# One-token attention and MLP on one core: values lag six units instead of five, mask added on VectorE, last batch summed in another PSUM bank, first w_2 group loaded in three pieces of rows

## The chip, the core and the metric

The kernel runs on one core of a Trainium2 chip. The time is device microseconds of one execution. The kernel before took 135.18 us as the median of three runs (134.91 to 135.40). Lower is better. All inputs start in HBM, and the output of 576 numbers ends there.

In the text PE is TensorE, DVE is VectorE, ACT is ScalarE, POOL is GpSimd, and SP is the engine that issues nearly all of the DMAs here.

## The reference

One token x of 576 numbers goes through two branches that a scalar gate mixes.

```
g = sigmoid(sum(x * gate_w))
q = x @ wq                                   # 32 heads of 128
k, v = last 4096 positions of the caches     # 16 kv heads, each shared by 2 query heads
a = softmax(q k^T / sqrt(128)) v, heads side by side, @ wo
b = gelu(x @ w1 + b1) @ w2 + b2              # 576 -> 4608 -> 576
out = g * a + (1 - g) * b
```

Everything is bf16 in HBM. The windows of the k and v caches are 16.8 MB each, and wq, w1, wo and w2 have 4.7 to 5.3 MB each. One execution reads 53.6 MB.

## The kernel before, in words

**Units, batches, tiles.** There are 16 kv heads. One kv head (with its two query heads) is a *unit*, `h` in the code, and four units are a *batch* (`HB = 4`, `NB = 4`). A tile of keys or values holds two units in 2 MB. Two DMAs fill it, one into the even partitions and one into the odd ones (`load_kv`, line 99). Six such buffers exist (`kv_pool`, line 77), and keys, values and later the four groups of w_2 take them in turn. A load waits until the last reader of the buffer's earlier content is done.

**What one unit does.** `transposes(h, i)` (line 228) turns four 128x128 blocks of keys by four matmuls against the identity, for i = 0 to 7. They go to one of three PSUM banks (`ps_t`), and DVE (i = 0, 3, 6) or ACT copies them to SBUF. `scores(h, s)` (line 256) adds four matmuls at a time into the PSUM bank `s_ps`, which collects a whole batch. Partitions and columns of even and odd parity belong to different units, so half of the entries of `s_ps` mean nothing. Before, one matmul at the start of each batch (line 261) writes 0 or -1e30 into the bank as a mask, and the scores add to it. `values(h, i)` (line 330) multiplies the probabilities with the values and adds up a whole batch in the PSUM bank `acc` (`ps_o`, one bank).

**Once for a batch.** `softmax(b)` gives four steps: `row_max` (line 284, DVE), `turn_max` (two small DVE operations around a transpose on PE), `spread` (PE spreads the maximum, ACT takes the exponential out of `s_ps`), and `put` (four transposes and eight DVE copies into `ez`). `heads_out(b)` gives two: `take` (line 348, four DVE operations read `acc` and add its four blocks into `a_s`) and `turn_out` (one matmul and a copy into `o_sb`). `norm` (line 501) sums up the denominators, `sums_start` (line 522) clears the bank in which the output is added.

**The order.** The program is written in the order in which each engine runs it. The loop (line 535) goes over `h`. While unit h is scored, the keys of unit h + 1 are transposed, the softmax steps of a batch that has ended are put between them, and the values of unit h - LAG are multiplied, with LAG = 5 (line 531). The loop runs on for five rounds after the last unit, in which only values, the last softmax and the `heads_out` steps are left. `gelu` (line 459) runs as one block at the end of round 10.

**Loads.** SP issues the DMAs in the order of the program, with at most eight on their way: each DMA waits on a completion counter that the one eight places before it has used. The last in this order are eight of values, two of wo, and six of w_2. The four w_2 groups have 128 rows each, and each row of a group is one run of 10368 bytes in HBM. The last group goes in three pieces of columns (line 587).

**The end.** `ow` (lines 593 to 612) is the attention output as columns. The sums for the output (line 632) are 64 matmuls with wo, then 54 with the w_2 groups 0 to 2. `part_s` (line 640) takes them out of PSUM. The last matmuls (line 651) add them and w_2 group 3 into `y_ps`, `y` (line 664) casts the result, and one DMA of four rows writes it.

Of the kernel before, what the change touches and what calls it, by code (L numbers as in the profile page):

```python
# [16 lines left out]
def kernel(  # L17
# [15 lines left out]
    nc = tc.nc  # L33
# [131 lines left out]
    for o in range(2):  # L165
# [22 lines left out]
    row_e = const.tile([2, P], BF16, name="row_e")  # L188
    nc.vector.tensor_copy(
        out=row_e[:].rearrange("k (a e q) -> k a e q", e=2, q=2),  # L190
        in_=ident[0:2, 0:2].rearrange("k (a e q) -> k a e q", a=1, q=1).to_broadcast(
            [2, P // 4, 2, 2]
        ),
    )
    col_e = const.tile([2, BC * P], BF16, name="col_e")
    nc.vector.tensor_scalar(
        out=col_e[:].rearrange("k (a e) -> k a e", e=2),
        in0=ident[0:2, 0:2].rearrange("k (a e) -> k a e", a=1).to_broadcast([2, BC * P // 2, 2]),
        scalar1=-MASK, scalar2=MASK, op0=ALU.mult, op1=ALU.add,
    )  # L200

# [54 lines left out]
    def scores(h, s):  # L256

        b, ul = h // HB, h % HB
        if ul == 0 and s == 0:
            s_tiles[b] = ps_s.tile([P, BC * P], FP32, name="s_ps", tag="s")  # L260
            nc.tensor.matmul(
                s_tiles[b][:], lhsT=row_e[:], rhs=col_e[:], start=True, stop=False
            )
        lo = R * (NGR - 1 - 2 * (h % 2) - s)
        for t in range(NQ):
            i = 4 * s + t
            nc.tensor.matmul(  # L267
                s_tiles[b][32 * t : 32 * (t + 1), :],
                lhsT=qz[:, h // 2, lo : lo + 32],
                rhs=kT[h][:, i * BC * P : (i + 1) * BC * P],  # L270
                start=False,
                stop=(ul == HB - 1 and s == 1),
            )

    def softmax(b):

        s_ps = s_tiles[b]
        mx = small.tile([P, 1], FP32, name="mx", tag="mx")
        m8 = small.tile([1, R], FP32, name="m8", tag="m8")
# [4 lines left out]
        def row_max():  # L284
            nc.vector.tensor_reduce(out=mx[:], in_=s_ps[:], axis=AX.X, op=ALU.max)  # L285
# [12 lines left out]
        def spread():  # L298
            mb = ps_m.tile([P, 1], FP32, name="mb", tag="m")
            nc.tensor.matmul(mb[:], lhsT=m_all[:], rhs=ones_ff[0:1, 0:1], start=True, stop=True)  # L300
            nc.vector.tensor_scalar(  # L301
                out=nb[:], in0=mb[:], scalar1=-SCALE, scalar2=None, op0=ALU.mult
            )
            nc.scalar.activation(  # L304
                out=pr[:], in_=s_ps[:], func=ACT.Exp, bias=nb[:, 0:1], scale=SCALE,
                accum_out=sums[:, b : b + 1],
            )

        def put():
            pT = ps_m.tile([P, BC, P], BF16, name="pT", tag="m")  # L310
            for c in range(BC):
                nc.tensor.transpose(  # L312
                    out=pT[:, c, :], in_=pr[:, c * P : (c + 1) * P], identity=ident[:]
                )
            for s in range(NGR):
                for m in range(HB // 2):
                    nc.vector.tensor_copy(  # L317
                        out=ez[:, b % 2, m, NQ * s : NQ * (s + 1), :, RP * m : RP * (m + 1)],
                        in_=pT[:].rearrange("p c (t s r) -> p t c s r", t=NQ, r=R)[
                            :, :, :, s, RP * m : RP * (m + 1)  # L320
                        ],
                    )
# [7 lines left out]
    def values(h, i):  # L330

        b, ul = h // HB, h % HB
        if ul == 0 and i == 0:
            acc[b] = ps_o.tile([P, BC, Dh], FP32, name="acc", tag="o")
# [124 lines left out]
    def gelu():  # L459
        NF = RJ * NG  # L460
        C0 = 0.7978845608028654
        h_r = const.tile([P, 2, FB], FP32, name="h_r")
        nc.vector.tensor_tensor(
            out=h_r[:], in0=h_box[0][:, :, 0:FB], in1=b1_r[:], op=ALU.add
        )

        hT = ps_m.tile([P, RJ, NG], FP32, name="hT", tag="m")
        rows = h_r[:].rearrange("p k n -> p (k n)")
        for j in range(RJ):
            for e in range(2):  # L470
                nc.tensor.matmul(  # L471
                    hT[64 * e : 64 * (e + 1), j, :],
                    lhsT=rows[:, j : j + RJ * 63 + 1 : RJ],
                    rhs=sel_f[:, e, :],
                    start=True,
                    stop=True,
                )
        hacc = const.tile([P, NF], FP32, name="hacc")
        nc.vector.tensor_copy(out=hacc[:], in_=hT[:].rearrange("p j g -> p (j g)"))
        z2 = const.tile([P, NF], FP32, name="z2")  # L480
        nc.vector.tensor_tensor(out=z2[:], in0=hacc[:], in1=hacc[:], op=ALU.mult)
        poly = const.tile([P, NF], FP32, name="poly")
        nc.vector.tensor_scalar(
            out=poly[:], in0=z2[:], scalar1=2.0 * C0 * 0.044715, scalar2=2.0 * C0,
            op0=ALU.mult, op1=ALU.add,
        )
        u_t = const.tile([P, NF], FP32, name="u_t")
        nc.vector.tensor_tensor(out=u_t[:], in0=poly[:], in1=hacc[:], op=ALU.mult)
        e_t = const.tile([P, NF], FP32, name="e_t")
        nc.scalar.activation(out=e_t[:], in_=u_t[:], func=ACT.Exp, scale=-1.0)  # L490
        nc.vector.tensor_scalar(out=e_t[:], in0=e_t[:], scalar1=1.0, scalar2=None, op0=ALU.add)
        r_t = const.tile([P, NF], FP32, name="r_t")
        nc.vector.reciprocal(out=r_t[:], in_=e_t[:])
        nc.vector.scalar_tensor_tensor(
            out=gt[:].rearrange("p j g -> p (j g)"), in0=hacc[:], scalar=omg[:, 0:1], in1=r_t[:],
            op0=ALU.mult, op1=ALU.mult,
        )
# [31 lines left out]

    W1_AT = {1: 0, 5: 1, 9: 2}  # L530
    LAG = HB + 1
    OUT_AT = NU + 1
    chain, tail = [], []
    w1_ready = None
    for h in range(NU + LAG):
        if 1 <= h < NU - 3 and h % 2 == 1:
            k_tiles[(h + 3) // 2] = load_k((h + 3) // 2)
        if 0 <= h - HB < NU and h % 2 == 0:
            v_tiles[(h - HB) // 2] = load_v((h - HB) // 2)
# [8 lines left out]
        for i in range(NBL):  # L548
# [3 lines left out]
            at = (6, 7) if h % HB == 0 else (2, 5)  # L552
            if i in at and h < NU:
# [3 lines left out]
            if i in (0, 5) and tail:  # L557
                tail.pop(0)()
            if h >= LAG and i % 4 == 3:
                for j in range(i - 3, i + 1):  # L560
                    values(h - LAG, j)
        if h >= LAG and (h - LAG) % HB == HB - 1:
            tail = heads_out((h - LAG) // HB)
        if w1_ready is not None:
            w1_mul(*w1_ready)
            if w1_ready[0] == len(PIECES) - 1:
                gelu()
        w1_ready = w1_next
        if h % HB == HB - 1 and h < NU:
            chain = softmax(h // HB) + ([norm] if h == NU - 1 else [])  # L570
        if h == OUT_AT:
            sums_start()
    for f in tail:
        f()
# [10 lines left out]
    for g in range(NG):  # L585
        t = kv_pool.tile([P, NCK * Dh], BF16, name="w2_t", tag="kv")
        cut = (0, RJ) if g < NG - 1 else (0, 6, 8, RJ)
        for lo, hi in zip(cut, cut[1:]):
            nc.sync.dma_start(out=t[:, lo * D : hi * D], in_=w2_view[g, :, lo * D : hi * D])
# [8 lines left out]
    for j in range(OJ):  # L598
# [8 lines left out]
    ow_f = const.tile([P, OJ, NOG], FP32, name="ow_f")  # L607
    nc.vector.tensor_reduce(
        out=ow_f[:].rearrange("p j o -> p (j o)"), in_=ow_m[:], axis=AX.X, op=ALU.add
    )  # L610
    ow = const.tile([P, OJ, NOG], BF16, name="ow")
    nc.vector.tensor_copy(out=ow[:], in_=ow_f[:])  # L612
# [85 lines left out]
```

## Time and profile before

| what | value |
|---|---|
| three runs, us | 134.91, 135.18, 135.40 |
| the profiled execution's own time, us | 135.28 |
| its span, us | 133.4 |
| mean granted TensorE clock | 0.834 |
| busy PE / DVE / ACT, us | 93.8 / 61.0 / 48.4 |
| read from HBM, MB | 53.62 |
| mean rate of the DMAs, GB/s | 403 |

The span goes from the first to the last instruction of the profiled execution, and its own time has 1.88 us more, around the span. Times of day below are microseconds from the span's start. In the rows a "group" is all instructions of one line of the code on one engine, with the count after an x. In the chain of waits each row has a start, a duration and the work that the chain passes through in that time; "issue" means that the engine waited for nothing that the profile shows. In the rows of 40 slices each digit is the busy share of a slice in tenths, and PEclk is the clock granted to TensorE in tenths of full speed.

### The profile page before, as it was taken

Reading aid. Unit: us, or ns where it says so; the run is one execution under the profiler, and the core shown is the slowest. Engines: PE = TensorE matmul, PEld = TensorE weight load, DVE = VectorE, ACT = ScalarE, POOL = GpSimd, SP = SyncE. Lnnn points to the kernel's source line nnn. Section 1 sums busy time; section 2 is a strip of 40 time slices with the busy share of each in tenths; the row PEclk is TensorE's granted clock in tenths of the full one; section 3 lists DMA queues with packets and bytes.
Section 4 is the critical chain, followed back from the end, with each engine's and each line's share of the span. In section 5 each row is a group of like instructions: output and inputs, shape, how many; then the busy total and the mean of one; then the engine's idle time right before and its main releaser. Section 6 shows DMA issues by size and latency. Waiting matters only on the chain.

```text
span 133.4 us, 2689 instructions
## 1 busy us (share of the span) xinstructions
PE 93.8 (70%) x1131; PEld 59.6 (45%) x1131; DVE 61.0 (46%) x160; ACT 48.4 (36%) x91; POOL 4.2 (3%) x11
## 2 busy tenths in 40 slices
PE   0007985299495999199596978979999852936970
PEld 0007741267364665165454647547456421413540
DVE  4954632036248656022857653563474536253020
ACT  3003750066365777024564741436237520000000
POOL 8400000000000000000000000000000000000000
PEclk9999999657999999756999998555559995595599
DMA  3999999999999999999999999999999999999950
GB/s 79 423 443 420 437 425 447 413 439 420 440 418 442 413 435 414 455 413 442 418 425 437 418 432 427 437 418 432 432 427 437 401 428 437 426 426 432 408 206 5
DMA packets 4809, 53.79 MB, mean 403 GB/s; under 512 B 819, under 2 KB 958, under 8 KB 1342
## 3 DMA queue, kind: packets, MB, share of 16 engines
q1 hardware_dynamic: 4792, 53.62, 94.8%
q8 instruction: 9, 0.15, 0.4%
q14 instruction: 2, 0.02, 0.0%
q10 hardware_dynamic: 6, 0.00, 0.0%
HBM read 53.62 MB, written 0.00 MB: 402 GB/s over the span
## 4 chain that ended last, share of the span: by engine, by line
DMA 43%; PE 37%; DVE 13%; issue 2%; SPq 2%; ACT 1%; DVEq 0%; ACTq 0%
DMA v_t<-in_A_v_cache_dram 17%; DMA k_t<-in_A_k_cache_dram 14%; DMA wq_t<-in_A_wq_dram 12%; PE tp L233 12%; PE acc L337 8%; PE part L632 5%; PE s_ps L267 4%; DVE a_s L353 3%; DVE kT L242 2%; PE hT L471 2%; DVE mx L285 1%; PE o_ps L360 1%; PE pT L312 1%; PE mb L300 1%; SPq L102 1%
## 5 line engine op out<-in xcount | busy, mean ns | idle before, releaser
L244 ACT CAST kT<-tp 128x512 bf16<-128x512 f32 x80 | 43.9, 587 | 42.6 <-PE tp L233 42.3
L233 PE MATMUL tp<-ident,k_t 128*128 128x128 bf16 x512 | 47.5, 247 | 5.0 <-DMA k_t<-in_A_k_cache_dram 3.3
L242 DVE CAST kT<-tp 128x512 bf16<-128x512 f32 x48 | 32.9, 690 | 37.2 <-PE tp L233 32.5
L233 PEld LDWEIGHTS <-k_t 128*128 128x128 bf16 x512 | 37.2, 112 | 19.3 <-issue 18.4
L337 PE MATMUL acc<-v_t,ez 128*32 128x512 bf16 x128 | 14.5, 479 | 3.4 <-DVE a_s L353 3.1
L267 PE MATMUL s_ps<-kT,qz 128*32 128x512 bf16 x128 | 14.3, 440 | 0.0
L449 PE MATMUL h_ps<-w_t,x 128*32 128x288 bf16 x72 | 3.7, 356 | 4.8 <-DMA w_t<-in_B_w_dram 4.8
L337 PEld LDWEIGHTS <-ez 128*32 128x32 bf16 x128 | 3.7, 105 | 7.2 <-issue 3.3
L368 PE MATMUL x_ps<-x,dup 64*128 64x9 bf16 x1 | 0.2, 165 | 8.7 <-DMA x<-in_A_x_dram 8.7
L267 PEld LDWEIGHTS <-qz 128*32 128x32 bf16 x128 | 3.3, 95 | 4.8 <-issue 2.4
L449 PEld LDWEIGHTS <-x 128*32 128x32 bf16 x72 | 2.5, 115 | 5.6 <-issue 5.1
L317 DVE COPY ez<-pT 128x64 bf16<-128x64 bf16 x32 | 3.5, 181 | 3.2 <-PE pT L312 3.2
L632 PE MATMUL part<-wo_t,ow 128*1 128x288 bf16 x64 | 4.0, 443 | 1.2 <-DVE ow L612 1.2
L353 DVE SCALAR_TENSOR_TENSOR a_s<-acc,m_c,a_s 128x128 f32<-128x128 f32 x12 | 4.2, 351 | 0.4
L304 ACT ACTIVATE pr<-s_ps,nb 128x512 bf16<-128x512 f32 x4 | 2.7, 687 | 4.3 <-DVE nb L301 4.3
L640 DVE SCALAR_TENSOR_TENSOR part_s<-b_r,omg,part 128x576 f32<-128x576 bf16 x1 | 0.8, 816 | 7.0 <-PE part L632 7.0
L146 DVE CAST ident_f<-ident 128x128 f32<-128x128 bf16 x1 | 3.0, 3000 | 1.8 <-POOL ident masks.py:199 1.8
L289 PE MATMUL mT<-ident_f,mx 128*1 128x128 f32 x4 | 1.2, 296 | 3.5 <-DVE mx L285 3.5
L632 PE MATMUL part<-w_t,gt 128*1 128x288 bf16 x54 | 3.3, 378 | 0.0
L632 PEld LDWEIGHTS <-ow 128*1 128x1 bf16 x64 | 2.0, 121 | 2.7 <-DVE ow L612 1.3
L387 ACT ACTIVATE ge<-g_ps 128x1 f32<-128x1 f32 x1 | 0.2, 171 | 7.8 <-PE g_ps L385 7.8
L285 DVE TENSOR_REDUCE mx<-s_ps 128x1 f32<-128x512 f32 x4 | 2.7, 683 | 0.6 <-PE s_ps L267 0.6
(83 smaller groups left out, 49.9 us busy)
## 6 DMA issues: line engine op xcount, KB each, us to landing
k_t<-in_A_k_cache_dram SPq DMA_DIRECT2D x16, 1024.0 KB, 18.9
v_t<-in_A_v_cache_dram SPq DMA_DIRECT2D x16, 1024.0 KB, 18.4
wq_t<-in_A_wq_dram SPq DMA_DIRECT2D x2, 2304.0 KB, 13.7
w_t<-in_B_w_dram SPq DMA_DIRECT2D x2, 2304.0 KB, 22.0
wo_t<-in_A_wo_dram SPq DMA_DIRECT2D x2, 2304.0 KB
w_t<-in_B_w_dram SPq DMA_DIRECT2D x3, 1296.0 KB, 19.6
w_t<-in_B_w_dram SPq DMA_DIRECT2D x1, 864.0 KB
w_t<-in_B_w_dram SPq DMA_DIRECT2D x1, 576.0 KB, 18.3
```

The lines of the kernel that those rows point to most:

```text
L146: nc.vector.tensor_copy(out=ident_f[:], in_=ident[:])
L233: nc.tensor.matmul(tp[:, c * P : (c + 1) * P], lhsT=k_tiles[h // 2][:, (h % 2) * NCH + i * BC + c, :], rhs=ident[:], start=True, stop=True,)
L242: nc.vector.tensor_copy(out=dst, in_=tp[:])
L244: nc.scalar.copy(out=dst, in_=tp[:])
L267: nc.tensor.matmul(s_tiles[b][32 * t : 32 * (t + 1), :], lhsT=qz[:, h // 2, lo : lo + 32], rhs=kT[h][:, i * BC * P : (i + 1) * BC * P], st ...
L285: nc.vector.tensor_reduce(out=mx[:], in_=s_ps[:], axis=AX.X, op=ALU.max)
L304: nc.scalar.activation(out=pr[:], in_=s_ps[:], func=ACT.Exp, bias=nb[:, 0:1], scale=SCALE, accum_out=sums[:, b : b + 1],)
L317: nc.vector.tensor_copy(out=ez[:, b % 2, m, NQ * s : NQ * (s + 1), :, RP * m : RP * (m + 1)], in_=pT[:].rearrange("p c (t s r) -> p t c s ...
L337: nc.tensor.matmul(acc[b][32 * ct : 32 * ct + 4 * R, :, :], lhsT=ez[:, b % 2, ul // 2, n, :, :].rearrange("p c r -> p (c r)"), rhs=v_tiles ...
L353: nc.vector.scalar_tensor_tensor(out=a_s[:], in0=acc[b][:, c, :], scalar=m_c[:, c : c + 1], in1=a_s[:], op0=ALU.mult, op1=ALU.add,)
L449: nc.tensor.matmul(h_box[0][32 * t : 32 * (t + 1), k, 0:FB], lhsT=x2[:, m, :], rhs=w[:, off : off + FB], start=(m == 0), stop=(m == NM - 1),)
L632: nc.tensor.matmul(part[32 * t : 32 * t + 1, k, 0:DB], lhsT=col, rhs=w[:, i * D + k * DB : i * D + (k + 1) * DB], start=(n == 0), stop=(n ...
```

## The change

1. **Lag.** LAG goes from five units to six. The loop stops at the last unit, and what is left is written out behind it: row maximum, the values of unit 10, `turn_max`, the values of unit 11, `spread`, `put`, `take` and `turn_out` of batch 2 around the values of unit 12, `norm`, `sums_start`, the values of units 13 to 15, and `heads_out` of batch 3. The last two loads of values are issued behind the loop. `norm` stood before `take` of batch 2 and stands behind it now.
2. **Another bank.** The last batch's `acc` is one of the three banks of the key transposes. It no longer waits until `take` has read the bank of the batch before.
3. **Mask.** The mask matmul on PE is gone (four of them). A mask tile of 128x512 is built on DVE at the start, and the row maximum becomes one DVE operation that adds the mask to the scores, writes the sum to SBUF (`ms`) and gives its maximum. The exponential reads `ms`, no longer PSUM. The scores of a batch's first unit stand at steps 4 and 6 of the round instead of 6 and 7.
4. **GELU.** The same instructions, in eleven pieces over the first five steps of round 11 instead of in one block at the end of round 10.
5. **w_2.** Group 0 is loaded as 112 rows, then eight rows, then eight rows, each a DMA of its own.
6. **Small ones.** The eight copies of `put` go by half batch first. `ow` is written as bf16 by the reduction, without the copy behind it.

```diff
-    row_e = const.tile([2, P], BF16, name="row_e")
...
+    mask = const.tile([P, BC * P], BF16, name="mask")
+    for e in range(2):
+        nc.vector.tensor_copy(
+            out=mask[:, e::2], in_=row_e[:, e : e + 1].to_broadcast([P, BC * P // 2])
+        )
...
-            nc.tensor.matmul(
-                s_tiles[b][:], lhsT=row_e[:], rhs=col_e[:], start=True, stop=False
-            )
...
-                start=False,
+                start=(ul == 0 and s == 0),
...
-            nc.vector.tensor_reduce(out=mx[:], in_=s_ps[:], axis=AX.X, op=ALU.max)
+            nc.vector.tensor_tensor_reduce(
+                out=ms[:], in0=s_ps[:], in1=mask[:], scale=1.0, scalar=-3.0e38,
+                op0=ALU.add, op1=ALU.max, accum_out=mx[:],
+            )
...
-                out=pr[:], in_=s_ps[:], func=ACT.Exp, bias=nb[:, 0:1], scale=SCALE,
+                out=pr[:], in_=ms[:], func=ACT.Exp, bias=nb[:, 0:1], scale=SCALE,
...
-            acc[b] = ps_o.tile([P, BC, Dh], FP32, name="acc", tag="o")
+            pool, tag = (ps_t, "tp") if b == NB - 1 else (ps_o, "o")
+            acc[b] = pool.tile([P, BC, Dh], FP32, name="acc", tag=tag)
...
-    LAG = HB + 1
+    LAG = HB + 2
...
-    for h in range(NU + LAG):
+    for h in range(NU):
...
-            at = (6, 7) if h % HB == 0 else (2, 5)
+            at = (4, 6) if h % HB == 0 else (2, 5)
...
+            for f in (mlp[0:1], mlp[1:4], mlp[4:7], mlp[7:10], mlp[10:11])[i] if i < 5 else []:
+                f()
...
+    row_max, turn_max, spread, put = softmax(NB - 1)
+    for h in (NU, NU + 2):
+        v_tiles[(h - HB) // 2] = load_v((h - HB) // 2)
...
+    row_max()
+    unit(NU - LAG)
+    turn_max()
+    unit(NU - LAG + 1)
+    spread()
+    put()
+    take, turn_out = heads_out(NB - 2)
+    take()
+    unit(NU - HB)
+    turn_out()
+    norm()
+    sums_start()
+    for h in range(NU - HB + 1, NU):
+        unit(h)
+    take, turn_out = heads_out(NB - 1)
+    take()
+    turn_out()
...
-        for lo, hi in zip(cut, cut[1:]):
-            nc.sync.dma_start(out=t[:, lo * D : hi * D], in_=w2_view[g, :, lo * D : hi * D])
+        rows = (0, P) if g > 0 else (0, 112, 120, P)
+        for a, b in zip(rows, rows[1:]):
+            for lo, hi in zip(cut, cut[1:]):
+                nc.sync.dma_start(
+                    out=t[a:b, lo * D : hi * D], in_=w2_view[g, a:b, lo * D : hi * D]
+                )
...
-    ow_f = const.tile([P, OJ, NOG], FP32, name="ow_f")
...
-    nc.vector.tensor_copy(out=ow[:], in_=ow_f[:])
+            out=ow[:].rearrange("p j o -> p (j o)"), in_=ow_m[:], axis=AX.X, op=ALU.add
```

## The prediction, made before the changed kernel ran

> **What bounds the kernel now.** First I read the page's rows of slices.
>
> ```profile
> span 133.4 us, 2689 instructions
> PEclk9999999657999999756999998555559995595599
> DMA  3999999999999999999999999999999999999950
> GB/s 79 423 443 420 437 425 447 413 439 420 440 418 442 413 435 414 455 413 442 418 425 437 418 432 427 437 418 432 432 427 437 401 428 437 426 426 432 408 206 5
> ```
>
> The DMAs never pause until slice 38 (126.7 us). No rearrangement of engines can end before the loads do, so the question is how far PE is behind them. The chain of waits over the span ends so:
>
> ```profile
> 106.16 0.70 DVE mx L285
> ...
> 109.73 0.87 DVE ez L317 x8
> 110.61 0.11 DVE sg L504
> ...
> 110.86 0.62 PE t_ps L511 x2
> ...
> 111.50 0.36 DVE r_sums L514
> 111.86 0.18 DVE a_s L349
> ...
> 113.24 0.62 PE acc L337 x4
> 113.86 0.53 PE o_ps L360 x2
> 114.38 2.86 PE acc L337 x21
> ...
> 121.07 0.19 DVE ow L612
> 121.26 0.04 issue
> 121.31 7.13 PE part L632 x118
> 128.43 0.03 issue
> 128.46 0.83 DVE part_s L640
> 129.29 0.04 issue
> 129.33 1.01 PE y_ps L651 x44
> 130.36 0.31 DVE y L664
> ```
>
> From 106 us the end is the last batch's softmax, then `norm`, then `take` of batch 2, which holds the only `acc` bank until 113.2, then values, sums and output. No transfer is in it. I then looked at the DMA view of 104 to 134 us, in slices of 0.75 us:
>
> ```profile
> GB/s 359 436 406 393 430 430 455 418 406 430 442 430 442 418 410 455 455 401 429 429 429 429 429 415 429 429 442 446 382 369 421 329 217 85 0 22 0 2 0 0
> ```
>
> The rate halves at 128 us (217 against 430) before it stops: half of the 16 DMA engines run dry early. The trace's packet records (start, duration and size of each) show why. Each engine's packets follow one another without gaps, so completion writes can be followed engine by engine. At 23.5 us 15 of 16 are within 0.43 us. Then eight engines, one after another, carry one 16 KB packet of the instruction queue (at 23.8, 40.0, 50.8, 65.1, 77.5, 88.5, 105.2 and 124.8 us) and fall 1.4 us behind for good. The others finish their loads at 127.51 to 127.89, two at 128.24 and 128.42; these eight at 128.94 to 129.21.
>
> From a completion write to the PE instruction that waits for it, the records show 0.39 us (wq at 19.47), 0.42 (w_1 at 35.98) and 0.51 (w_1 at 56.19); I take 0.45. The last w_2 piece can so be multiplied from 129.21 + 0.45 = 129.66. Its four matmuls ran some 0.6 us later, at the end of the 1.01 us of y_ps. So PE is the bound, but by little: with PE out of the way the present loads would give back only about 0.4 us.
>
> **The change part by part.**
>
> *Mask.* Four mask matmuls go: on the chain 0.33 us at 67.9 and 0.54 at 93.3, in all 0.87 us (the first two lie before 56.2, where PE waited 3.0 us for w_1 anyway). The new row maximum is not in the trace. Nearest rows: the 128x512 reduction, 0.683; the 128x576 addition out of PSUM to fp32, 0.758, which for 512 is about 0.69; and 0.07 for reading the accumulator as a row of its own. Bounds -0.02 and +0.15; I take +0.08, three times on the chain. The exponential reads SBUF instead of PSUM; no such row, taken at 0 with 0.1 either way of its 0.687. Building the mask costs a reduction (0.26 to 0.36), a small operation (0.15) and two copies of 128x256 (a quarter of the 1.04 of the 1024-element copy each) minus 0.34 for the two operations removed: +0.6 us on DVE at 7 us. It is hidden by DVE's 1.47 us of idleness before the x columns at 9.02; without that cover wq (last needed at 19.47) hides it still.
>
> *GELU.* The block held PE for 0.92 us (h_r), then, behind 2.33 us of matmuls, 0.50 more, because ACT stood 4.2 us at `e_t` and its key copies behind it. Spread out, the matmuls stay, a wait for h_r stays (key copy 0.69 + h_r 0.76 on DVE), the second wait can go. I take 0, bounds -0.5 and +0.6.
>
> *Lag.* In rounds 8 to 15 as many values are multiplied as before. What is late next: buffers come free one round later. Values tile 3 then is issued near 64 us for 75, values tile 6 near 88 for 94; w_2 group 0 near 102 instead of 97.7 for 115. The tightest issue is values tile 7, waiting for key tile 6 as now: SP issued it at 95.3, its packets started at 99.2. So the loads keep flowing. The two extra w_2 DMAs use two of eight places in flight; the last piece then waits for the second wo load (lands 116.8) and is needed by 128. Their issue, about 0.4 us each, has that cover. Hidden: 0.
>
> *Tail.* Leaving the loop's end at 105.86. Row maximum to 106.95; the transpose to 107.27; values of unit 11 (8 x 0.102, from 2.86 us for 28) cover the small DVE operations and push `spread` 0.25 later than 107.89; exponential and `put` then end at 110.85, half of `ez` at 110.45. Unit 12 starts there in the new bank, not at 113.24. `take` runs 110.9 to 112.35, o_ps, its copy, `sg` and t_ps end at 113.75, and 24 matmuls of units 13 to 15 (2.45) at 116.2 instead of 117.25: 1.05 us. The removed copy of `ow` gives 0.21. So `ow` is ready at 120.0. Then 64 wo matmuls to 124.0, and the w_2 groups follow at 1.1 us each; group 2 has landed on the last engine at 126.04 - 0.39 + 0.45 = 126.1, so part ends at 127.2 whether or not the loop gains its 0.87. Before: 128.43.
>
> *w_2 group 0.* A row of 10368 bytes takes 0.389 us on an engine. 112 rows are seven an engine. The two b_1 loads of four rows show four completion writes each, not 16, so a load of eight rows runs on eight engines, and both on the same ones if the four are a guide: these get nine rows, the other eight seven. The four engines with b_1 packets are all among the early eight. If the early eight are the low ones, the late ones end at 129.21 - 0.39 = 128.83, and the early ones at 128.42 + 0.40 = 128.82 at most. Bounds: 128.83 and, if the extra rows meet a late engine, 129.61. I take 128.83, for b_1's sake.
>
> [...]
>
> *The sum.* part 127.2, `part_s` to 128.07, its eight matmuls and the w_2 pieces that have landed until 128.95; the last piece is ready at 128.83 + 0.45 = 129.28, its four matmuls (226 ns, nearly together) with the step to DVE take 0.29, so `y` starts at 129.57 instead of 130.36: -0.79 us. From the profiled execution's 135.28 that makes 134.5. That execution is 0.1 above the median, so against 135.18 it makes 134.4.
>
> **The rivals.**
>
> *A, the row split meets the wrong engines.* [...] Then the last piece lands at 129.61, multiplied from 130.06, `y` at 130.35: 135.2. Against it: all four b_1 engines are early, for which a random choice has 7 in 100 (126 of 1820).
>
> *B, the split evens out nothing, PE is ahead.* For it: engines fall behind by when the instruction packets come, and one more DVE packet (8 KB, 0.6 to 0.85 us at 49.2 and 68.7, both on early engines) could hit another. The loads end at 129.21 as now: `y` at 129.95, 134.8.
>
> *C, slower: TensorE's clock.* In the loop one stretch is at half speed, seen in two windows:
>
> ```profile
> 84.00:90.00 6.00, 5.05 (x41) 2.99 (x41) 3.08 (x6) 2.24 (x4) 0.00 (x0) 0.50 1.02 431
> 90.00:96.00 6.00, 6.00 (x47) 3.45 (x45) 2.80 (x13) 3.02 (x6) 0.00 (x0) 0.50 1.01 431
> ```
>
> (The column before the last two is the clock.) Round 12 took 8.6 us there against 6.0 for its like, round 8; round 11 took 5.9 against 3.4 for round 14. So each 6.8 us more of half clock between 57 and 105 costs about 2.5 us. The PE chain has 0.3 us of room before the loads' end (127.5 against 127.2), 1.2 with the mask's gain; to be slower than before by 0.3% it must lose some 1.5 us more. One stretch more gives 135.6 to 136.5, the higher with the mask's gain lost too; I say 135.9. If it comes before round 12, values tile 7 is issued too late as well. Against it: the stretch of 17 us already in the loop began at 82.7, behind the GELU block's 36 matmuls of four columns and its waits, which are now spread; it can as well shorten, and then nothing changes, as the loads set the end.
>
> [...]
>
> **How the numbers follow.** A measurement of this kernel can tell about 0.3%, 0.41 us, so faster means under 134.77. The forecast, loads at the end and evened out, has 0.66 (134.1 to 134.75 by the bounds of 0.1 to 0.3 us above); A 0.13, the same; B 0.08, half faster and half the same; C 0.13, slower. Faster 0.68, same 0.17, slower 0.15, with 0.02 from the forecast for a late issue on SP. The range goes from 134.1 to 135.4: it holds the forecast, B and A, and leaves out C.
>
> **What would show it.** Right: in the slices of 0.75 us no stretch at half rate at the end, loads over by about 128.8; PE's last four y_ps matmuls waiting for the w_2 load; acc of the last batch starting within 0.1 us of the first `ez` copies, no `sg` in front of it; no L261 row; the new row maximum at 0.7 to 0.85. Wrong: the half-rate stretch grown to 2 us (A), half clock longer than 17 us between 57 and 105 (C), a slice of the page under 400 GB/s before 126 us (a late issue), or `part` starting after 120.5.

## The result, and the profile after

The kernel after took 140.84 us (140.29 to 140.88, four runs) against 135.17 us for the kernel before on the same chip: ratio 1.0401, 95% interval 1.0367 to 1.0436. The prediction said 134.4 us, with a range up to 135.4. The profiled execution took 140.29 us, with a span of 138.4 us.

The page of the kernel after, the rows of 40 slices (3.46 us each) that the prediction read first:

```profile
span 138.4 us, 2689 instructions
...
PEclk9999999559999999599599995555999855568555
DMA  2999999999999999999999999999999999999940
GB/s 86 446 417 426 426 450 407 445 418 436 436 431 417 436 421 429 426 445 417 429 440 410 438 431 426 426 426 431 436 431 400 432 429 325 246 192 418 413 152 0
```

The DMA engines are busy throughout, but in slices 34 to 36 (114 to 125 us) they move 325, 246 and 192 GB/s instead of 430: busy, and half as fast. The DMA view of 104 to 139 us, in slices of 0.875 us, gives the stretch more closely:

```profile
GB/s 356 407 421 432 463 390 463 400 463 390 453 411 438 357 191 201 273 261 213 201 178 261 201 273 422 462 391 399 423 431 421 370 283 78 1 19 0 1 0 0
```

Ten slices, from 116.25 to 125.0 us, have a mean of 225 GB/s. That is 8.75 us x (430 - 225) GB/s = 1.79 MB too little, or 4.2 us at full rate. The packet records agree: half of the w_2 packets of 10368 bytes that start in this stretch take 669 to 786 ns (median 752) instead of 389, and wo's last packets (9216 bytes, 347 ns elsewhere) take 667 to 704. The first w_2 packet starts at 115.06 us, and slow ones start from 115.6 on. The stretch lasts as long as any engine is in one of the three loads of w_2 group 0: it ends at 125.0, and PE starts the matmuls of that group at 125.41. All data is in SBUF at 133.81 us, before the change at 129.21. The chain of waits ends so (start, duration, work; for a DMA the time from its issue to its landing):

```profile
105.40 25.73 DMA w_t<-in_B_w_dram
...
131.17 1.61 PE part L674 x18
...
132.80 0.82 DVE part_s L682
...
133.67 1.76 PE y_ps L693 x44
...
135.45 0.31 DVE y L706
```

Before, no transfer was in this part of the chain; now one of w_2 holds 25.73 us of it. PE's timeline shows the same from its side (start, duration, work, and in brackets the idle time before it and what ended that):

```profile
125.41 0.90 PE L674 MATMUL part<-w_t,gt 128*1 128x288 bf16 x18 [1.79 <-DMA w_t<-in_B_w_dram]
128.07 1.60 PE L674 MATMUL part<-w_t,gt 128*1 128x288 bf16 x18 [1.76 <-DMA w_t<-in_B_w_dram]
131.17 1.60 PE L674 MATMUL part<-w_t,gt 128*1 128x288 bf16 x18 [1.50 <-DMA w_t<-in_B_w_dram]
```

PE, which set the end before, waits for each of the three w_2 groups.

### The profile page after: what moved, and what is told of

It reads as the page before. It is cut to its first block, busy times and chain, and to the rows that moved or that the text cites. A ratio compares the mean times of both kernels' runs of the same rounds, so it can differ in the third digit from the quotient of the medians.

```text
span 138.4 us, 2689 instructions
## 1 busy us (share of the span) xinstructions
PE 94.0 (68%) x1127; PEld 60.0 (43%) x1127; DVE 61.4 (44%) x165; ACT 48.8 (35%) x91; POOL 4.2 (3%) x11
## 4 chain that ended last, share of the span: by engine, by line
DMA 54%; PE 35%; DVE 7%; issue 1%; DVEq 0%
DMA w_t<-in_B_w_dram 36%; DMA k_t<-in_A_k_cache_dram 18%; PE tp L233 17%; PE s_ps L264 5%; PE acc L340 5%; DVE kT L242 3%; PE hT L479 2%; PE h_ps L452 2%; DVE a_s L356 2%; PE y_ps L693 1%; PE part L674 1%; DVE ms L283 1%; PE pT L313 1%; PE mb L301 1%; DVE part_s L682 1%
## 5 line engine op out<-in xcount | busy, mean ns | idle before, releaser
L340 PE MATMUL acc<-v_t,ez 128*32 128x512 bf16 x128 | 13.4, 462 | 2.4 <-DVE a_s L356 2.1
L674 PE MATMUL part<-w_t,gt 128*1 128x288 bf16 x54 | 4.1, 384 | 5.1 <-DMA w_t<-in_B_w_dram 5.1
L674 PEld LDWEIGHTS <-gt 128*1 128x1 bf16 x54 | 2.0, 98 | 7.2 <-issue 3.8
L305 ACT ACTIVATE pr<-ms,nb 128x512 bf16<-128x512 f32 x4 | 2.9, 722 | 4.3 <-DVE nb L302 4.3
L363 PE MATMUL o_ps<-m_r,a_s 128*128 128x8 f32 x8 | 1.9, 315 | 3.2 <-DVE a_s L356 3.2
L363 PEld LDWEIGHTS o_ps<-m_r,a_s 128*128 128x128 f32 x8 | 1.6, 248 | 4.9 <-DVE a_s L356 2.5
L479 PE MATMUL hT<-sel_f,h_r 128*64 128x4 f32 x36 | 2.7, 265 | 1.3 <-DVE h_r L470 1.3
```

Source lines behind the costliest of these rows:

```text
L340: nc.tensor.matmul(acc[b][32 * ct : 32 * ct + 4 * R, :, :], lhsT=ez[:, b % 2, ul // 2, n, :, :].rearrange("p c r -> p (c r)"), rhs=v_tiles ...
L363: nc.tensor.matmul(o_ps[:], lhsT=a_s[:], rhs=m_r[:], start=True, stop=True)
L479: nc.tensor.matmul(box[0][64 * e : 64 * (e + 1), j, :], lhsT=rows[:, j : j + RJ * 63 + 1 : RJ], rhs=sel_f[:, e, :], start=True, stop=True,)
L674: nc.tensor.matmul(part[32 * t : 32 * t + 1, k, 0:DB], lhsT=col, rhs=w[:, i * D + k * DB : i * D + (k + 1) * DB], start=(n == 0), stop=(n ...
```

## The experiments

All edits are made to the kernel after unless said otherwise, and all times stand beside runs of the kernel before on the same chip.

### Is it the row split? (one load again; the split alone)

```diff
-        rows = (0, P) if g > 0 else (0, 112, 120, P)
+        rows = (0, P) if g > 0 else (0, P)
```

> The changed kernel with w_2 group 0 loaded as one DMA of 128 rows again; all else as changed. In the changed kernel's trace the DMAs' rate falls to about 200 to 270 GB/s from 115.3 to 123.8 us, just when the 112-row load starts. Theory 1 (the row split causes the fall): the rate stays above 400 GB/s until 126 us, packets of 10368 bytes take 0.389 us throughout, the loads end near 129.2, y starts near 129.95, and the time is about 134.8 (0.3% below before). Theory 2 (something else in the change, such as the new order of the tail or later issues, slows the DMAs): the fall stays and the time is about 140.8.

Measured: 135.1 us (134.74 to 135.75), ratio 0.9993 (0.9969 to 1.0016). The DMA view of 104 to 139 us and the end of the chain:

```profile
GB/s 460 334 432 442 421 442 421 442 400 453 400 453 406 460 425 403 427 474 415 403 438 450 410 415 399 399 407 261 163 25 0 1 0 0 9 9 0 0 0 0
```

```profile
107.94 21.89 DMA w_t<-in_B_w_dram
...
129.87 0.26 PE y_ps L693 x4
...
130.16 0.31 DVE y L706
```

The slow stretch is gone. The last load (129.53) ends the chain, and only the last four matmuls follow it, as the prediction had drawn its end.

The second edit adds only the row split to the kernel before:

```diff
-        for lo, hi in zip(cut, cut[1:]):
-            nc.sync.dma_start(out=t[:, lo * D : hi * D], in_=w2_view[g, :, lo * D : hi * D])
+        rows = (0, P) if g > 0 else (0, 112, 120, P)
+        for a, b in zip(rows, rows[1:]):
+            for lo, hi in zip(cut, cut[1:]):
+                nc.sync.dma_start(
+                    out=t[a:b, lo * D : hi * D], in_=w2_view[g, a:b, lo * D : hi * D]
+                )
```

> The kernel before with nothing changed but w_2 group 0 loaded as 112, 8 and 8 rows. Theory 1 (the row split alone): the same fall of the rate and packets of about 0.78 us, loads over near 134, time 139.5 to 141. Theory 2 (the split is harmless without the other parts): about 135.2, or 0.4 less if the engines are evened out.

Measured: 139.98 us (139.53 to 140.59), ratio 1.0355 (1.0286 to 1.0423); the last data lands at 133.86. The split is enough by itself and it is needed: it carries the whole loss. The five other parts are worth nothing that this measurement can tell.

### The source or the place in SBUF?

Two halves of 64 rows, into neighbouring partitions:

```diff
-        rows = (0, P) if g > 0 else (0, 112, 120, P)
+        rows = (0, P) if g > 0 else (0, 64, P)
```

And the same halves of the source, into the even and then the odd partitions, with this beside the line above:

```diff
+            to = t[a:b] if g > 0 else t[a // 64 : P : 2]
...
-                    out=t[a:b, lo * D : hi * D], in_=w2_view[g, a:b, lo * D : hi * D]
+                    out=to[:, lo * D : hi * D], in_=w2_view[g, a:b, lo * D : hi * D]
```

> The changed kernel with w_2 group 0 as two loads of 64 rows, into partitions 0 to 63 and 64 to 127. Each of 16 engines gets four rows, so no load runs on fewer engines. Theory S (engines that write into the same block of eight partitions slow one another; in a 128-row load each engine has a block of its own, in this one two engines share one): packets of 10368 bytes at about 0.6 to 0.8 us in group 0, time 136.5 to 139. Theory K (the two eight-row loads on eight engines are the cause): full rate, about 134.8. Theory H (the source addresses in HBM are the cause): slow too, and the next kernel likewise.

> As the kernel with two loads of 64 rows, from the same HBM rows in the same order, but into the even and then the odd partitions, as keys and values are loaded; so w_2 rows of group 0 meet the wrong gelu columns and the output is not the reference's. Theory S (shared blocks of partitions): full rate, packets 0.389 us, about 134.8. Theory H (source addresses in HBM): the same time as the kernel with contiguous halves. Theory K (eight-row loads): about 134.8.

Measured: 140.51 us (139.63 to 141.18), ratio 1.0394 (1.033 to 1.0459), for neighbouring partitions; 134.86 us (134.71 to 135.67), ratio 0.9989 (0.9965 to 1.0013), for every second one. The DMA view of the first and then of the second, 104 to 139 us:

```profile
GB/s 345 439 390 453 411 432 432 411 453 400 463 400 486 188 223 211 190 249 190 213 213 237 225 320 433 391 403 438 442 387 404 413 277 167 7 19 0 1 0 0
```

```profile
GB/s 348 418 432 421 432 421 453 411 453 411 432 421 440 436 435 415 438 438 415 415 433 427 403 407 427 413 396 245 115 19 0 1 0 0 19 0 0 0 0 0
```

Each run has two loads of 64 rows, by the count four for each engine, from the same addresses in HBM. Only the partitions differ, and they decide between half and full rate; theory H, the source addresses, falls. The first time lies 1.5 us above theory S's range. The prediction counted rows per engine, which are equal here.

### Eight-row loads, or the 112 rows?

```diff
-        rows = (0, P) if g > 0 else (0, 112, 120, P)
-        for a, b in zip(rows, rows[1:]):
+        rows = [slice(0, P)] if g > 0 else [slice(0, 112), slice(112, P)]
+        for r in rows:
...
-                    out=t[a:b, lo * D : hi * D], in_=w2_view[g, a:b, lo * D : hi * D]
+                    out=t[r, lo * D : hi * D], in_=w2_view[g, r, lo * D : hi * D]
```

> The kernel after, with the two loads of eight rows joined into one of 16 rows, so that group 0 is loaded as 112 rows and 16 rows, each an equal number of rows for every engine (seven and one). Theory A: the 112-row load alone, seven neighbouring rows for an engine and so rows that do not begin at multiples of eight partitions, halves the rate; it carries seven eighths of the group, so most of the loss stays: slices at 180 to 310 GB/s for 6 to 9 us, time 138 to 140.8. Rival B: only the two loads of eight rows are to blame, which run on eight engines; then the 112-row load runs at 389 ns a packet, at most the one load of 16 rows slows, and the time is 135 to 136.5.

Measured: 140.53 us (140.0 to 140.89), ratio 1.0406 (1.0364 to 1.0448), slices of 118 to 296 GB/s from 116 to 125 us. No load of eight rows is left, and the loss is the same. That alone does not clear the load of 16 rows, which go to 16 neighbouring partitions. The packet records do: packets are slow from 115.1 us on, 0.4 us after the first one of the group, and followed from packet to packet the first engine ends its seven rows only at 119.4. For over 4 us the 112-row load alone runs at half rate, beside the last of wo. That much of theory A holds; its reason, blocks of eight partitions, is tested next.

### Loads with a stride

These runs cut group 0 by slices `r` of rows, each to its own partitions. First 64, 32, 16 and 16 rows:

```diff
-        rows = (0, P) if g > 0 else (0, 112, 120, P)
-        for a, b in zip(rows, rows[1:]):
+        rows = [slice(0, P)] if g > 0 else [slice(0, P, 2), slice(1, P, 4), slice(3, P, 8), slice(7, P, 8)]
+        for r in rows:
...
-                    out=t[a:b, lo * D : hi * D], in_=w2_view[g, a:b, lo * D : hi * D]
+                    out=t[r, lo * D : hi * D], in_=w2_view[g, r, lo * D : hi * D]
```

> The changed kernel with w_2 group 0 in four loads of 64, 32, 16 and 16 rows, with strides of 2, 4, 8 and 8 partitions, so that each of the 16 engines has all of its rows inside the block of eight partitions that it has in a 128-row load. Theory A (the rate falls for all engines while any engine writes outside its own block of eight): full rate, packets 0.389 us, about 134.9. Theory N (several smaller loads as such, or rows that don't follow one another, cost the time): slower, 137 to 141.

Measured: 136.96 us (136.53 to 137.6), ratio 1.0124 (1.007 to 1.0178). Packets of the 64- and 32-row loads took 389 ns until the first engines came to the 16-row loads; from about 118 to 121.5 us, with these two loads, the slices fell to 213 to 344 GB/s. Full rate throughout, as theory A had it, failed, and 137 us or more, as theory N had it, was not quite reached.

The last 16 rows as twice eight (in this excerpt and the next two the loop over `r` and the load are as above):

```diff
+        rows = [slice(0, P)] if g > 0 else [slice(0, P, 2), slice(1, P, 4), slice(3, P, 8), slice(7, 64, 8), slice(71, P, 8)]
```

> As the kernel with four strided loads, but the last 16 rows as two loads of eight rows with a stride of eight partitions. [...] That is the evening-out of nine and seven rows without the 112-row load. Theory A: half rate while the second eight rows are written, which with the engines' spread of 1.7 us is a loss of 0.5 to 1.5 us: 135.2 to 136.4. Theory E (evening out works where the rows are few): loads end 0.39 us earlier than with four strided loads, 134.5.

Measured: 136.89 us (136.78 to 137.59), ratio 1.0126 (1.0078 to 1.0173): no difference from the run with 16 rows. It is above the range of theory A, and theory E's evening-out of nine and seven rows (134.5) did not come. Both took the two loads to run on the same eight engines, and theory A the second eight rows to lie outside those engines' blocks; no record names the engines of these loads.

Four loads of 32 rows, each within one half of the partitions:

```diff
+        rows = [slice(0, P)] if g > 0 else [slice(0, 64, 2), slice(1, 64, 2), slice(64, P, 2), slice(65, P, 2)]
```

> The changed kernel with w_2 group 0 in four loads of 32 rows at a stride of two partitions, two in partitions 0 to 63 and two in 64 to 127, so two rows an engine, four partitions apart, most of them outside the engine's own block of eight. Theory A: half rate from the first to the last of these rows, as with contiguous halves, 139 to 141. Theory D (it is neighbouring partitions within one load that cost the time, as the 112-row and the 64-row loads have them, and not the place of an engine's rows): full rate, about 134.9.

Measured: 139.51 us (139.45 to 139.6), ratio 1.0309 (1.0268 to 1.035), slices of 201 to 332 GB/s for some 8 us. A stride alone does not help these loads, whose rows stay in one half of the partitions.

64, 32 and 32 rows:

```diff
+        rows = [slice(0, P)] if g > 0 else [slice(0, P, 2), slice(1, P, 4), slice(3, P, 4)]
```

> The kernel after, with w_2 group 0 in three loads: every second row (64 rows), every fourth from row 1 (32 rows), every fourth from row 3 (32 rows). Compared with the four-load version of 64, 32, 16 and 16 rows (136.96 us, slow from about 118.3 to 121.9 us), the two loads of 16 rows, one row for each engine, have become one load of 32, two rows for each engine. Theory A: what slows the engines there is a load with a single row for each engine; then all 10368-byte packets take 389 ns, no slice between 104 and 126 us falls under 380 GB/s, and the time is 134.7 to 135.4. Rival B: it is loads of fewer than 64 rows, or the number of loads of one group, whatever the rows of an engine; then the slices fall to 210 to 310 GB/s while the 32-row loads run, for 2 us or more, and the time is 136.2 to 137.5.

Measured: 134.92 us (134.67 to 135.23), ratio 0.9982 (0.996 to 1.0003), every slice from 106 to 126 us at 386 GB/s or more. 16 rows with stride eight are slow where 32 with stride four are not.

Last, behind a single load of group 0, one load of 16 rows that nobody needs:

```diff
+            again = const.tile([P, 7 * D], BF16, name="again")
+            nc.sync.dma_start(out=again[3::8, :], in_=w2_view[0, 3::8, 0 : 7 * D])
```

> The kernel after with w_2 group 0 in one load of 128 rows, and behind it one more load, of nothing that is needed: 16 rows (3, 11, 19 ... of group 0, seven of nine column blocks, 8064 bytes each) into the same partitions of a tile that nobody reads, one row for each engine. At the full rate of 389 ns for 10368 bytes it costs each engine 0.30 us. Theory A: a load with one row for each engine slows all 16 engines while any engine is in it, as the two loads of 16 rows did (2.0 us for two, against the version with 32 rows in their place); then the slices from about 118 to 121 us fall to 230 to 330 GB/s for at least 1.5 us, packets of 10368 bytes take over 450 ns beside it, and the time is 135.8 to 136.8. Rival B: such a load is harmless alone, and what was slow came from group 0 being in four loads or more; then every 10368-byte packet takes 389 ns outside the fetches, and the time is that of the single load and 0.3 us more, 135.1 to 135.6.

Measured: 136.65 us (136.43 to 137.26), ratio 1.0135 (1.0089 to 1.018). From 119.0 to 121.5 us w_2 packets of 10368 bytes took mostly 490 to 600 ns beside it. So one load of 16 rows slows engines that are not in it at the time, and the number of loads is not the cause.

By now "each engine in its own block of eight partitions", which the strided halves had suggested, had fallen. It cannot explain the 16 rows. That an engine has such a block was assumed; no record here names the partition or the engine of a packet.

### Which partitions?

What the halves and the strided loads leave is theory P of the next expectations: the set of partitions that the rows of a load reach decides, whichever engines carry them. That 0 to 63 goes at about half rate the halves of 64 rows had shown (188 to 320 GB/s); that 32 to 95, 33, 37 ... 93 and 0, 4 ... 28 go at full rate was the author's assumption. Four loads of rows that nobody needs set it against the other readings. Each stands where the 16 extra rows stood:

```diff
-            nc.sync.dma_start(out=again[3::8, :], in_=w2_view[0, 3::8, 0 : 7 * D])
+            nc.sync.dma_start(out=again[32:96, :], in_=w2_view[0, 32:96, 0 : 7 * D])
```

The three others have `0:64`, `33:96:4` and `0:32:4` in both places: the same number of neighbouring rows 32 partitions further down, 16 rows with stride four instead of eight, and eight rows with stride four. For rows 32 to 95 theory P has full rate, which is an estimate of 1.21 us on top of the 135.1 of the single load: 136.3.

> The kernel after with w_2 group 0 in one load of 128 rows, and behind it a load of nothing needed: 64 neighbouring rows, 32 to 95 (8064 bytes each), into the same partitions of a tile that nobody reads. At 0.30 us a row it costs each engine 1.21 us if nothing slows. [...] Rival O (each engine must stay in its own block of eight neighbouring partitions): it is as slow as the halves of 64 neighbouring rows were, 190 to 250 GB/s for 2.4 us or more, 137.3 to 139 us.

> As the run with rows 32 to 95, with 64 rows 0 to 63 in their place: the same number of rows, neighbours too, the same bytes. [...] Theory P and rival O agree here: about half the rate (190 to 250 GB/s) while they run, 2.4 us or more instead of 1.21, and 137.3 to 139 us. If it is as fast as the other one, both fall.

Measured: 136.61 us (135.96 to 137.21), ratio 1.0069 (1.0032 to 1.0106), for rows 32 to 95; 139.37 us (139.24 to 139.97), ratio 1.0238 (1.0176 to 1.0301), for rows 0 to 63. The DMA view of the first and then of the second:

```profile
GB/s 382 397 463 379 463 390 474 400 453 421 432 432 423 412 483 386 431 406 475 421 403 433 462 379 411 442 406 392 273 182 23 0 1 0 0 19 0 0 0 0
```

```profile
GB/s 418 397 400 432 421 432 432 421 442 421 432 432 425 421 440 450 398 263 237 259 234 194 249 457 391 379 450 434 391 409 403 282 187 26 19 0 0 1 0 0
```

The same number of neighbouring rows and the same bytes; 32 partitions further up there is no slow slice, and all 64 packets take 305 ns. At 0 to 63 their median is 563 ns, and w_2 packets of 10368 bytes beside them take about 720. Rival O falls with the first run, which has the time of full rate. The second time lies 0.4 us above the range of both theories: the slow stretch lasted six slices, 5.25 us, not 2.4. That the engines come to the load at different times (in the kernel before they ended 1.7 us apart, at 127.51 to 129.21) may be a part of that, which is not shown.

> As the run with 16 extra rows 3, 11, 19 ... (136.65 us, slow from 119.0 to 121.5 us), with rows 33, 37, 41 ... 93 in their place: again 16 rows, one for each engine. [...] Theory P: full rate, all 10368-byte packets at 389 ns outside the fetches, and 0.30 us more than the single load: 135.1 to 135.6 us. Rival S (a load with a single row for each engine is slow wherever its rows go): as before, 136.2 to 137 us.

> As the runs with extra rows, with eight rows: 0, 4, 8 ... 28. [...] Theory P: full rate, 134.8 to 135.5 us. Rival S2 (a load that runs on eight engines is slow in itself): 230 to 340 GB/s around 119 us for a microsecond or more, 135.8 us or above. Besides, the engines that finish last show where small loads go: if the eight early engines carry them, the last w_2 packet ends where it does without them, at 129.1 to 129.6 us; if late ones do, 0.3 us later.

Measured: 135.28 us (135.12 to 135.61), ratio 0.995 (0.9926 to 0.9974), for 16 rows with stride four, against 136.65 us with stride eight; 135.3 us (135.03 to 136.07), ratio 0.9975 (0.9942 to 1.0007), for eight rows. All extra packets took 305 ns in both. So neither a load of 16 rows nor one of eight is slow in itself, and rivals S and S2 fall. The last run's data was in at 129.58 us, which does not tell which engines took the eight rows: the runs without extra rows end between 129.1 and 129.5 anyway.

The kernel before was at 135.76 us in this comparison, so the ratios below 1 are no gain: a single load without extra rows took 135.1. Theory P told right from wrong rows in all four runs. All pieces and extra loads, by what was measured:

| partitions | what was measured |
|---|---|
| 0 to 127 | 389 ns a packet of 10368 bytes in the kernel before; 135.1 us as a single load in the kernel after |
| 0, 2 ... 126, then 1, 3 ... 127 | no slice under 403 GB/s from 105 to 126 us, 134.86 us |
| 0, 2 ... 126, then 1, 5 ... 125, then 3, 7 ... 127 | no slice under 386 GB/s from 106 to 126 us, 134.92 us |
| 32 to 95 (extra) | 305 ns a packet of 8064 bytes, 136.61 us |
| 33, 37 ... 93 (extra) | 305 ns, 135.28 us |
| 0, 4 ... 28 (extra) | 305 ns, 135.3 us |
| 0 to 63, then 64 to 127 | 188 to 320 GB/s, 140.51 us |
| 0, 2 ... 62, then 1, 3 ... 63, then the same from 64 | 201 to 332 GB/s, 139.51 us |
| 0 to 63 (extra) | 563 ns, 194 to 263 GB/s, 139.37 us |
| 0, 2 ... 126, then 1, 5 ... 125, then 3, 11 ... 123, then 7, 15 ... 127 | 213 to 344 GB/s with the last two, 136.96 us |
| 3, 11 ... 123 (extra) | 490 to 600 ns a packet of 10368 bytes beside it, 136.65 us |
| 0 to 111, then 112 to 127 | 118 to 296 GB/s, 140.53 us |

So the place in SBUF is shown to decide. What the sets at full rate have in common is not shown, and in what order the engines take the rows, no record shows either.

The 112-row load is the hardest to place: neighbouring rows from one end of the partitions almost to the other, as in the load of 128, seven for each engine by the count instead of eight, and yet packets with a median of 752 ns instead of 389 in the kernel after. That the 112 rows halve the rate is measured; why they halve it stays open.

### What the other parts are worth to PE

The second wo load is left out, so that the loads end 5.5 us sooner; in its place the first wo tile is multiplied, so the attention half of the output comes from wrong weights. Once in the kernel before, once in the kernel after with one load for group 0:

```diff
-    for i in range(NOG // 2):
+    for i in range(1):
...
         wo_t.append(t)
+    wo_t.append(wo_t[0])
```

> The kernel before, without the second wo load (the first wo tile stands in its place in the matmuls, so the attention branch's half of the output is computed from the wrong weights; everything else stays). The loads end some 5.5 us sooner (2.36 MB at 430 GB/s). It measures how far PE alone is. If the prediction's reading is right that PE sets the end of the kernel before by 0.4 us at most, y comes at 130.2 to 130.4 as before and the time is 134.8 to 135.2. Rival: the loads set its end, or their traffic slows PE; then it is under 134.5.

> The kernel after with group 0 in one load of 128 rows, and without the second wo load (the first wo tile stands in its place, so the attention branch's part of the output comes from the wrong weights). With the loads out of the way it shows what the lag, the other bank, the mask and the spread GELU give PE. By the prediction's steps for the tail (ow ready at 120.0, 118 matmuls in 7.13 us, part_s 0.83, y_ps 1.01 at the clock of before) y comes at 129.0 and the time is 133.9; if y_ps runs at half clock, as in the kernel after, 1.76 instead of 1.01, it is 134.6. Rival: the edits give PE nothing; then the time is that of the kernel before with the same load left out, within 0.3%.

Measured: 135.19, 135.59, 136.09 and once 130.08 us for the first (granted clock 0.844 to 0.858, and 0.903 in the last); 131.46 us (130.97 to 132.67) for the second. The ends of the two chains, first the kernel before without the load:

```profile
122.04 6.27 PE part L633 x118
...
129.21 1.01 PE y_ps L652 x44
130.24 0.31 DVE y L665
```

```profile
118.79 6.05 PE part L675 x118
...
125.74 1.01 PE y_ps L694 x44
...
126.77 0.31 DVE y L707
```

In these two executions (135.19 and 131.83 us) PE starts the output 3.25 us sooner after the change and ends 3.5 us sooner. That is no measure of the other parts: the kernel before has one run of 130.08, shorter than all four of the kernel after (130.97 to 132.67), so the old order can do it too, and a gain for PE is not shown. Nor would the whole kernels show one, since the loads end at 129.1 to 129.5 either way. Three of the four runs of the kernel before end as if nothing had been left out, which agrees with the prediction's reading that PE set its end; the fourth ends where its rival had it. My expectation of 133.9 for the second missed by 2.4: it kept the 7.13 us of the 118 matmuls, which were partly at half clock, and an `ow` ready 1.2 us later.

## Why the prediction was wrong

**w_2 group 0: the step that failed.** It said "112 rows are seven an engine", priced a row at 0.389 us wherever it goes, and bounded the end of the loads by 128.83 and 129.61. They ended at 133.81: the pieces ran at half rate, and the two halves of 64 rows show that their partitions can do that with everything else equal. The 0.389 us was read from loads of 128 rows, and the step carried it over to pieces of 112 and eight. In the slow stretch a row took about 0.75 us, and the rate of all 16 engines together fell to 178 to 273 GB/s, also of those in other loads (wo's last packets took 667 to 704 ns instead of 347). The bounds moved rows between engines, and no bound asked whether a row keeps its price at other partitions. Every large load of the kernel before is spread evenly from partition 0 to 127 (all of them, or every second one for keys and values), so no row of its trace could show the price of another place; the step should have said so and kept a wide upper end. From the last packet of w_2 group 2 (130.63) the chain then runs through its 18 matmuls, `part_s` and `y_ps`, the first and the last of them at half clock (1.61, and 1.76 where it was 1.01), and `y` starts at 135.45 instead of 130.36.

The 128.83 in the sum also needed the eight-row loads to run on the eight early engines ("If the early eight are the low ones"). No run shows that: no record numbers the engines or says which of them carried these loads. Nor did the loss hang on loads of eight rows, since 112 and 16 rows lost as much (140.53 us).

**Mask: within its bounds.** The row maximum was taken 0.08 us dearer. The kernel after, line 283 (count, then minimum, median and maximum in ns):

```profile
L283 DVE CUSTOM_DVE_ANT_0 ms<-s_ps,mask x4: 681/681/692, 41.1 to 105.2; 128x512 f32<-128x512 f32 x4
L283 DVE DVE_READ_ACCUMULATOR2_ANT mx<- x4: 83/83/84, 41.7 to 105.8; 128x1 f32 x4
```

That is 0.681 + 0.083 against 0.683, but the second row does not come on top. The chain of the kernel before, and then of the kernel after with one load of group 0:

```profile
106.16 0.70 DVE mx L285
...
106.90 0.28 PE mT L289
```

```profile
105.46 0.69 DVE ms L283
...
106.22 0.27 PE mT L290
```

From the start of the row maximum to the transpose behind it are 0.76 us, against 0.74 before. On the chain it costs 0.02, not 0.08. The exponential out of SBUF takes 0.722 us instead of 0.687, inside the 0.1.

**GELU: within its bounds.** The wait for `h_r` is 1.29 us instead of 0.92, and the second wait of 0.50 is gone: -0.13 in these waits, inside "-0.5 and +0.6".

**Lag: right.** Up to 114 us no slice of the page but the first is under 400 GB/s. The loads kept flowing.

**Tail: the right time, in part by luck.** PE's timeline of the kernel after with one load of group 0:

```profile
109.33 0.62 PE L340 MATMUL acc<-v_t,ez 128*32 128x512 bf16 x8 [0.28 <-DVE ez L318]
...
119.87 4.01 PE L674 MATMUL part<-wo_t,ow 128*1 128x288 bf16 x64 [0.97 <-DVE ow L652]
```

Unit 12 starts when the first `ez` copies are there and not behind `sg`, at 109.33 (forecast 110.45, before 113.24), and the wo matmuls at 119.87 (forecast 120.0, before 121.31). But the row maximum starts at 105.46 instead of 106.16: the loop ended 0.70 us sooner, where the forecast had left its end as it was. Counted from there, the wo matmuls start 14.41 us later, against 13.84 in the forecast and 15.15 before. The tail itself gave 0.74 us of the 1.31 forecast, and the loop's gain hid the rest. TensorE's clock was at half from 110.2 to 123.9 in this execution and at full from 116.8 to 120.2 in the one before (the last two `o_ps` matmuls took 0.59 us here and 0.39 there); whether that took the rest is not shown.

**The sum and the rivals.** Without the row split's places, what is left is rival B, in which the loads end as before and PE is ahead: it gave 134.8, and the kernel with a single load took 135.1, with its loads ending at 129.53 instead of 129.21. So even the forecast's gain, 0.8 us, would have needed an evening-out of engines that no run achieved. A was wrong in kind: the rows did cost, but not by meeting late engines. Its chance was also miscounted: all four b_1 engines among the eight early ones are 70 cases of 1820, 4 in 100, not 126 and 7. C did not come: in the loop the long half-clock stretch was 13.7 us (82.7 to 96.4) against 17.0 before. The sign went wrong by a mechanism that none of the rivals had.

## What to carry to other kernels

Before a DMA is cut along the partitions, work out which partitions each piece reaches, not only how many rows: pieces of 64 or 16 rows ran at full rate (430 GB/s) or at 190 to 340 by their position and stride alone. A duration read from loads that are spread over all 128 partitions need not hold for a piece that lies elsewhere. The runs give a list of places and no reason behind it, so a piece at a place that no run has shown is best measured. Transfers beside a slow piece slow as well (packets of 10368 bytes took 490 to 600 ns beside 16 extra rows and about 720 beside 64, instead of 389), so even a small piece near the end of a kernel that the loads bound is dear: with 16 extra rows the kernel took 136.65 us at stride eight and 135.28 at stride four.

## What the runs showed of the hardware that I had not expected

- Where 64 extra rows (0.52 MB) go in SBUF is worth 2.8 us: 139.37 us for partitions 0 to 63, 136.61 for 32 to 95.
- One load in the wrong partitions slows the others: w_2 packets of 10368 bytes went from 389 to about 720 ns while 64 rows of another tile were written to partitions 0 to 63.
- DMA engines are shown as nine tenths busy or more while they move 192 to 325 GB/s instead of 430 (slices 34 to 36 of the kernel after). Busy share does not tell the two apart; GB/s and the duration of one packet (389 or about 750 ns) do.
- The kernel before without 2.36 MB of its loads took 135.19 to 136.09 us in three runs, with the granted clock at 0.844 to 0.858, and 130.08 in one, with the clock at 0.903.
